# A second group of three tiles and a last unit of seven, in a chunked-attention and maxout kernel

## The chip, the cores and the metric

The kernel runs on one core of one Trainium2 chip. Its time is the device time of one execution in microseconds (us), as the median of several runs. TensorE (PE) multiplies, VectorE (DVE), ScalarE (ACT) and GpSimd (POOL) do the elementwise work, and SyncE (SP) issues every transfer between HBM and the on-chip memory. Each engine works through its own list of instructions in order and waits at an instruction until what that instruction needs is there.

## The reference

The inputs are q, k, v of shape (8, 8, 576, 64) and four weights. Attention runs inside chunks of 64 rows; its output becomes 4608 rows of 512, which go through a maximum of three products and a last product:

```python
scores = scale * np.matmul(q_c, k_c.transpose(0, 1, 2, 4, 3))   # chunks of 64
scores = scores - np.max(scores, axis=-1, keepdims=True)
attn = np.exp(scores)
attn = attn / (np.sum(attn, axis=-1, keepdims=True) + 1e-09)
x = np.matmul(attn, v_c)                        # then laid out as 4608 x 512
h = np.maximum(np.maximum(x @ w1, x @ w2), x @ w3)     # 512 -> 768
out = h @ w_out                                        # 768 -> 512
```

## The kernel before

The 4608 rows are 36 tiles of 128. The first eight tiles are two plain groups of four (`GROUPS = [4, 4]`); the other 28 are four units of 6, 8, 8 and 6 tiles (`UNITS`). Every fp32 product is made of three matmuls on a high and a low part of each operand (`three`, lines 173 to 176).

A plain group makes 18 products (six column blocks j of the 768, three weights w), each 4 x 3 matmuls of 128 x 512, and then projects each tile with 6 x 3 matmuls of 128 x 512. A unit multiplies by Winograd's form of Strassen's rule: 7 block products where the plain way has 8. Per unit there are 9 sets (three pairs of j, three w) of 7 products of 2 x 3 matmuls, and 7 x 2 x 3 x 3 matmuls of projection, 504 in all, each as wide as half a unit: 384 columns for six tiles, 512 for eight.

The units need weights that are mixed beforehand, once: for each of the 9 sets GpSimd adds the high and low parts back together (`f`, two instructions on line 370) and makes four sums and differences (`c`, four instructions on line 383); ScalarE casts `c` to its high part (`s`, line 388), VectorE makes the low part (line 391), and two transfers write `s` to HBM (line 405). The mixing runs beside the end of the first group and the whole second group. `f` and `c` have one buffer each, so a set's first `c` waits until VectorE has read the last one's.

When the second group's 18 products are done, the early pools are given up (`change`), and the memory that held weights and `s` holds the units' operands: X1 to X7 (line 503 the high part on ScalarE, line 507 the low part on VectorE, lines 498 the mixes), the sums `kept`, and the ring of weights loaded back from HBM (line 529). The first write of X1 therefore waits for the last transfer of mixed weights.

Attention is spread between the matmuls: S (scores, line 227), T (transposes, line 253) and V (values, line 265) of later tiles are inserted on TensorE; the softmax between them runs on VectorE, ScalarE and, in the last insertion of a stretch, GpSimd (line 191 divides by the sum; T waits for it).

The order is set in two ways. `FIRST` is a list written by hand for the first group (M in it starts the clock of the mixing). From there on a planner counts a nominal time `now` along TensorE's steps, and everything else is put down with a due time by `plan` and is emitted when `now` has passed it. The due times only set the order on each engine; on the chip an instruction runs when its waits are over.

Of the kernel before, what the change touches and what calls it, by code (L numbers as in the profile page):

```python
# [9 lines left out]
F32 = mybir.dt.float32  # L10
# [10 lines left out]
P = 128  # L21
# [3 lines left out]
SCALE = 1.0 / float(D) ** 0.5  # L25
GROUPS = [4, 4]
UNITS = [6, 8, 8, 6]
PAIRED = sum(GROUPS)
HALF = 512
# [6 lines left out]
OPERANDS = 0.94  # L36
MIX = 0.52

# [17 lines left out]
X51 A52 Y50p W65 K11 exp6 B60 A61 Y42 F32f h40f hh3f nrm5 h41f B63 C52 H51 V4 S7 A60 hl3f sum6 Y51 v6 W62 C60 F40f mx7  # L56
C61 X52p T5 X60 h42f H52 X61 H60 A62 xh4 h50f eps6 h51f Y60 K00 Y52p F41f A64 F42f P10 K12 hh4f H61 at5 C62 C64 K01
A63 xl4 h52f sub7 X64 B65 hl4fp K22 B62 exp7 P30 Y61 C63 V5 rec6 F50f X63p nrm6p T6 sum7 eps7 P20 K20 F51f X62p A65
rec7 C65 F52f P31 hh5f H62 xh5 v7 nrm7p Y62 at6 H63 hl5fp P21 Y63 T7 P22 P00 H64 K10 P23 P32 xl5 P01 X65 M at7 H65 P11
V6 V7 q8 q9 P12 xh6 xh7 xl6 P02 Y64 P13 xl7 Y65 P33 P34 P14 P35 P24 P03 P25 P04 K21 O2 P15 P05 K02 O0 O3 O1  # L60
"""
# [3 lines left out]
def chunk_attn_maxout_kernel(  # L65
# [48 lines left out]
    for name in FIRST.split():  # L114
        k = (3 * int(name[1]) + int(name[2])) if name[0] in "WAXY" else None
        if name[0] == "W":
            words_in[k] = free.pop(0)
# [86 lines left out]
    def plain_steps(t, x_of, col):  # L204
# [83 lines left out]

    def moe(t0, x_of, banks_in=((ps_m, "pm"),)):

# [57 lines left out]
        def hidden(j, w):  # L348
            for ct, _ in enumerate(products(j, w, 0, 512)):
                yield [] if ct < CT - 1 else [(0.3, lambda: maximum(j, w, 0, 512))] + (  # L350
                [(2.08, lambda: high(j, 0, 512)), (2.13, lambda: low(j, 0, 512))] if w == 2 else [])

# [7 lines left out]
    def store(n):  # L360
# [42 lines left out]
        def mixed():  # L403
            for k in range(2):
# [68 lines left out]
    def unit(t0, count, rooms):  # L473
# [35 lines left out]
        def operands():  # L509
            return [(0.0, high(1)), (0.39, low(1)), (2.71, mix(5, b12, b11, nc.vector)), (3.48, high(5)),  # L510
                    (3.31, mix(6, b22, source[5], nc.vector)), (8.01, mix(7, b22, b12, nc.gpsimd)), (3.37, high(6)),
                    (7.69, low(6)), (7.41, high(2)), (7.89, low(5)), (10.85, mix(4, b21, source[6], nc.gpsimd)), (7.67, low(2)),
                    (8.42, high(7)), (8.79, low(7))]

# [74 lines left out]
        def hidden(n, loads):  # L589
# [31 lines left out]
            if w == 2:  # L621
# [17 lines left out]
                def less(eng, out, x, y):  # L639
# [9 lines left out]
                             (5.31 * f, high(7)), (6.98 * f, low(7)), (6.27 * f, high(6)), (7.95 * f, low(6)),  # L649
                             (7.98 * f, high(4)), (8.86 * f, low(4))]  # L650
            for i in ORDER:
# [75 lines left out]
    idle = hpool.tile([P, 1024], mybir.dt.bfloat16, name="h", tag="h5")  # L727
    g0 = moe(0, lambda: x_tiles(0))
# [5 lines left out]
    for t in range(8):  # L734
        ops.update((f"{n}{t}", fn) for n, fn in plain_steps(t, lambda i=t // 4: x_tiles(i), t % 4 * P).items())
    for c, (lo, hi) in columns.items():
# [10 lines left out]
    mixing = [store(n) for n in range(len(sets))]  # L747
    for t in (8, 9):
        begun[t] = plain_steps(t, stage, (t - 8) * P)
        ops[f"q{t}"] = begun[t]["q"]  # L750

# [265 lines left out]
```

## Time and profile before

| | |
|---|---|
| three runs | 613.76, 614.07, 614.53 us, median 614.07 |
| profiled execution | 614.42 us, of which the span of the engines is 612.6 |
| TensorE | 605.4 us busy, 99% of the span, 5107 matmuls |
| VectorE, ScalarE, GpSimd | 432.5, 271.4, 291.1 us busy |
| granted TensorE clock | 1.0 of full speed over the span |

The profile is of one execution. Times in it count from the start of the span. TensorE's busy time is modelled at the ends of matmuls, so a step is read from the distance of two starts, not from the duration of one. The chain of waits goes back from the last instruction to whatever released each one; where it runs through other engines for a while, TensorE had no slack against them there, or nearly none.

In the profile's time the first group ends at 94.2 us, the second group's products at 154.2, its projection at 171.5, and the units fill the rest.

### The profile page before, as it was taken

What the parts mean: (1) busy time and instruction counts of PE and PEld (TensorE: products, weight loads), DVE (VectorE), ACT (ScalarE), POOL (GpSimd) and SP (SyncE); (2) the same over time, 40 slices, a digit from 0 to 9 for tenths busy, and PEclk for the clock granted to TensorE, in tenths of its full rate; (3) what the DMA queues carried; (4) which work ended last, traced back from release to release, by engine and by line L of the source; (5) the groups of instructions that cost most, each with busy time, mean ns of one, the idle gap of its engine ahead of it and who ended that gap; (6) DMA issues with size and microseconds to landing.
All of it is one profiled execution on the core that took longest, in us unless ns stands there. A gap on an engine that the chain in (4) does not pass through costs nothing.

```text
span 612.6 us, 12709 instructions
## 1 busy us (share of the span) xinstructions
PE 605.4 (99%) x5107; PEld 526.5 (86%) x5107; DVE 432.5 (71%) x678; ACT 271.4 (44%) x483; POOL 291.1 (48%) x241
## 2 busy tenths in 40 slices
PE   8999999999999999999999999999999999999997
PEld 4788888888899999998888887888888888999997
DVE  5899954687657988794595859863868387375752
ACT  5888643344444554544252535432434252242440
POOL 3553478884257775454262624532534234242430
PEclk9999999999999999999999999999999999999999
DMA  8986849687988997889585748497566657977774
GB/s 320 359 336 207 286 162 355 240 306 274 346 311 294 345 365 270 287 299 353 187 287 178 276 152 278 156 331 285 175 200 207 201 173 260 324 251 243 242 231 177
DMA packets 54219, 161.26 MB, mean 263 GB/s; under 512 B 4880, under 2 KB 16144, under 8 KB 49168
## 3 DMA queue, kind: packets, MB, share of 16 engines
q1 hardware_dynamic: 54160, 160.45, 74.6%
q8 instruction: 40, 0.66, 0.4%
q14 instruction: 19, 0.16, 0.1%
HBM read 128.97 MB, written 31.46 MB: 262 GB/s over the span
## 4 chain that ended last, share of the span: by engine, by line
PE 88%; DVE 4%; DMA 3%; ACT 2%; issue 1%; POOL 0%; SPq 0%; ACTq 0%; POOLq 0%; DVEq 0%
PE pm L586 65%; PE pm L174 5%; PE pm L175 5%; PE pm L176 5%; DMA buf<-in_qk 2%; PE s L227 2%; PE s L265 1%; PE y L265 1%; DMA w<-s 1%; PE y L227 1%; PE s L253 1%; PE tp L253 1%; PE y L253 1%; PE pm L755 1%; ACT X L503 1%
## 5 line engine op out<-in xcount | busy, mean ns | idle before, releaser
L586 PE MATMUL pm<-X,ring 128*128 128x512 f32 (+1 forms) x1512 | 310.9, 364 | 0.2 <-ACT kept L600 0.2
L586 PEld LDWEIGHTS pm<-X,ring 128*128 128x128 f32 x1512 | 271.3, 188 | 30.5 <-ACT kept L600 0.5
L600 ACT COPY kept<-pm 128x384 f32<-128x384 f32 (+1 forms) x108 | 57.1, 533 | 139.3 <-PE pm L586 101.2
L586 PE MATMUL pm<-Y,ring 128*128 128x512 f32 (+1 forms) x504 | 103.2, 363 | 0.1
L586 PEld LDWEIGHTS pm<-Y,ring 128*128 128x128 f32 x504 | 90.6, 188 | 10.4 <-DVE Y L636 0.6
L610 POOL TENSOR_TENSOR kept<-kept 128x384 f32<-128x384 f32 (+1 forms) x36 | 45.4, 1262 | 79.7 <-ACT kept L600 79.6
L597 DVE TENSOR_TENSOR most<-pm,most 128x384 f32<-128x384 f32 (+1 forms) x72 | 44.9, 623 | 51.7 <-PE pm L586 50.3
L191 POOL TENSOR_TENSOR e<-e,sm 128x512 f32<-128x512 f32 x27 | 31.8, 1177 | 62.9 <-DVE sm L188 44.2
L174 PE MATMUL pm<-xh,wl 128*128 128x512 f32 (+1 forms) x156 | 59.8, 383 | 0.0
L175 PE MATMUL pm<-xl,wh 128*128 128x512 f32 (+1 forms) x156 | 58.5, 375 | 0.3 <-DVE xl L276 0.3
L176 PE MATMUL pm<-xh,wh 128*128 128x512 f32 (+1 forms) x156 | 58.3, 373 | 0.0
L606 POOL TENSOR_TENSOR kept<-kept 128x384 f32<-128x384 f32 (+1 forms) x24 | 29.6, 1235 | 57.9 <-DVE kept L603 49.4
L636 DVE TENSOR_TENSOR Y<-most,Y 128x384 fp32r<-128x384 f32 (+1 forms) x72 | 53.7, 762 | 3.4 <-ACT Y L633 3.2
L633 ACT CAST Y<-most 128x384 fp32r<-128x384 f32 (+1 forms) x72 | 40.1, 570 | 30.3 <-DVE most L597 16.0
L241 ACT ACTIVATE e<-e 128x512 f32<-128x512 f32 x36 | 22.7, 631 | 34.4 <-DVE e L237 34.2
L603 DVE TENSOR_TENSOR kept<-pm,kept 128x384 f32<-128x384 f32 (+1 forms) x36 | 22.4, 621 | 18.3 <-PE pm L586 15.2
L603 DVE TENSOR_TENSOR pm<-pm,kept 128x384 f32<-128x384 f32 (+1 forms) x48 | 30.2, 628 | 7.1 <-PE pm L586 5.6
L175 PEld LDWEIGHTS pm<-xl,wh 128*128 128x128 f32 x156 | 29.4, 188 | 5.4 <-DVE xl L276 0.5
L176 PEld LDWEIGHTS pm<-xh,wh 128*128 128x128 f32 x156 | 29.4, 188 | 5.3
L174 PEld LDWEIGHTS pm<-xh,wl 128*128 128x128 f32 x156 | 29.4, 188 | 5.2
L182 DVE TENSOR_REDUCE sm<-e 128x8 f32<-128x512 f32 x36 | 24.5, 682 | 9.3 <-ACT e L241 8.7
L370 POOL TENSOR_TENSOR f<-wh,wl 128x512 f32<-128x512 f32 x18 | 27.3, 1539 | 2.5 <-DVE ao L163 1.8
(111 smaller groups left out, 843.7 us busy)
## 6 DMA issues: line engine op xcount, KB each, us to landing
ring<-w SPq DMA_DIRECT2D x36, 1024.0 KB, 5.5
ring<-w SPq DMA_DIRECT2D x36, 768.0 KB, 5.8
ring<-wo SPq DMA_DIRECT2D x28, 768.0 KB, 4.9
buf<-in_qk SPq DMA_DIRECT2D x36, 512.0 KB, 6.5
buf<-in_vb SPq DMA_DIRECT2D x36, 256.0 KB, 5.0
w<-s SPq DMA_DIRECT2D x18, 512.0 KB, 4.5
out_t<-ao SPq DMA_DIRECT2D x16, 256.0 KB, 3.9
stage<-in_w SPq DMA_DIRECT2D x7, 512.0 KB, 6.2
```

The costliest lines, as they stand in the source:

```text
L174: nc.tensor.matmul(out=o, lhsT=al, rhs=bh, start=first, stop=False)
L175: nc.tensor.matmul(out=o, lhsT=ah, rhs=bl, start=False, stop=False)
L176: nc.tensor.matmul(out=o, lhsT=ah, rhs=bh, start=False, stop=last)
L191: eng.tensor_tensor(out=e, in0=e, in1=sm.unsqueeze(2).broadcast_to([P, 8, 64]), op=ALU.mult)
L586: nc.tensor.matmul(out=o[i], lhsT=a, rhs=b, start=new and k == 0, stop=last and k == 2, skip_group_check=i in banks_of_product)
L597: return lambda: nc.vector.tensor_tensor(out=M(k, c), in0=of(), in1=M(k, c), op=most)
L600: return lambda: nc.scalar.copy(out=kept(k), in_=o[i])
L603: return lambda: nc.vector.tensor_tensor(out=out(), in0=o[i], in1=kept(k), op=plus)
L606: nc.gpsimd.tensor_tensor(out=kept(1) if w else M(1, 1), in0=kept(3), in1=kept(1), op=plus)
L610: (0.0, lambda: nc.gpsimd.tensor_tensor(out=kept(2), in0=kept(2), in1=kept(0), op=plus))],
L633: return lambda: nc.scalar.copy(out=y_room(i, jp)[:, 0, :half], in_=t[i]())
L636: return lambda: nc.vector.tensor_tensor(out=y_room(i, jp)[:, 1, :half], in0=t[i](), in1=y_room(i, jp)[:, 0, :half].bitcast(F32), op=minus)
```

## The change

One tile goes from the second group to the last unit: groups of 4 and 3, units of 6, 8, 8 and 7. The second group's products are then 384 columns wide and its projection has three tiles. Tile 7 keeps its attention in the first group and goes straight into the first unit's stage; the scores of tiles 8 and 9 move from the second group into the first (`S8 S9` behind `P33`), and their softmax with them.

The mixing of set 0 (`G0` to `G8`) stands in `FIRST` now, and M comes earlier. `f` and `c` have two places each, for even and odd sets. The planned distance of sets goes from 6.94 to 6.6, and within a set the high part, low part and store from 4.86, 5.79 and 8.77 to 9.0, 10.0 and 12.6. The second group has three insertions with values, of which the third lies ahead of the end of the products. The operands of the first unit have new due times, X2 early. Two loads of the projection's weights go to other buffers.

```diff
-GROUPS = [4, 4]
-UNITS = [6, 8, 8, 6]
+GROUPS = [4, 3]
+UNITS = [6, 8, 8, 7]
 # FIRST, one line of it before and after
-rec7 C65 F52f P31 hh5f H62 xh5 v7 nrm7p Y62 at6 H63 hl5fp P21 Y63 T7 P22 P00 H64 K10 P23 P32 xl5 P01 X65 M at7 H65 P11
+rec7 C65 F52f P31 hh5f H62 xh5 v7 nrm7p G2 G3 Y62 at6 H63 hl5fp G4 G5 M P21 Y63 T7 P22 P00 H64 K10 P23 P32 xl5 P01 X65 at7 H65 G6 P11
...
-            st["s"] = s = home(PAIRED)[:, :, t % 2 if t < 6 else 0]
+            st["s"] = s = (bank_of("ps_s") if t == 8 else home(PAIRED))[:, :, t % 2 if t < 6 else int(t == 8)]
...
         def hidden(j, w):
-            for ct, _ in enumerate(products(j, w, 0, 512)):
+            n = count * P
+            for ct, _ in enumerate(products(j, w, 0, n)):
...
-                    st["f"] = att.tile([P, 2, CT, P], F32, name="f", tag="qs", bufs=1)
+                    st["f"] = (att if n % 2 else xp).tile([P, 2, CT, P], F32, name="f", tag=("f", "qs")[n % 2], bufs=1)
...
-                    st["c"] = att.tile([P, 4, 256], F32, name="c", tag="rv", bufs=1)
+                    st["c"] = (att if n % 2 else xp).tile([P, 4, 256], F32, name="c", tag=("c", "rv")[n % 2], bufs=1)
...
-                (3.79, sum_of(3, a12, sums(0), minus)), (4.86, high), (5.79, low), (8.77, mixed)]
+                (3.79, sum_of(3, a12, sums(0), minus)), (9.0, high), (10.0, low), (12.6, mixed)]
...
     def stores():
-        for n in range(len(sets)):
+        for n in range(1, len(sets)):
             for at, fn in mixing[n]:
-                plan(now + MIX + 6.94 * n + at, 0.0, fn)
+                plan(now + 2.0 + 6.6 * (n - 1) + at, 0.0, fn)
...
     def first_tiles(time):
-        own, nexts = [[]] + pairs[0], pairs[0] + [pairs[1][0]]
-        lead = 8.84
-        gap = (time - lead - 0.5) / (len(own) - 1)
-        for i, (values, scores) in enumerate(zip(own, nexts)):
+        chain = [(8.84, [1, 2], [3, 4]), (24.6, [3, 4], [5]), (time - 4.9, [5], pairs[1][0])]
+        for n in (1, 2):
+            transposes(n, now + 4.0 + 0.7 * n)
+        for at, values, scores in chain:
...
-    parts += [("steps", lambda: g["project"](0, 1)), ("steps", lambda: g["project"](2)), ("steps", lambda: g["project"](3))]
+    parts += [("steps", lambda: g["project"](0, 1)), ("steps", lambda: g["project"](2))]
```

GpSimd at the end of the first group, before: the last low part of a group's `h`, then the first two sets.

```order
L325 TENSOR_TENSOR h<-m,h 128x512
L163 TENSOR_TENSOR ao<-ao,stage 128x512
L191 TENSOR_TENSOR e<-e,sm 128x512
L163 TENSOR_TENSOR ao<-ao,stage 128x512
L191 TENSOR_TENSOR e<-e,sm 128x512
L325 TENSOR_TENSOR h<-m,h 128x512
L370 TENSOR_TENSOR f<-wh_114,wl_120 128x512
L370 TENSOR_TENSOR f<-wh_115,wl_121 128x512
L383 TENSOR_TENSOR c<-f 128x256
```

The same place in the changed kernel:

```order
L372 TENSOR_TENSOR f<-wh_114,wl_120 128x512
L372 TENSOR_TENSOR f<-wh_115,wl_121 128x512
L326 TENSOR_TENSOR h<-m,h 128x512
L164 TENSOR_TENSOR ao<-ao,stage 128x512
L192 TENSOR_TENSOR e<-e,sm 128x512
L164 TENSOR_TENSOR ao<-ao,stage 128x512
L192 TENSOR_TENSOR e<-e,sm 128x512
L385 TENSOR_TENSOR c<-f 128x256
L385 TENSOR_TENSOR c<-c,f 128x256
L326 TENSOR_TENSOR h<-m,h 128x512
L385 TENSOR_TENSOR c<-f 128x256
L385 TENSOR_TENSOR c<-f,c 128x256
```

Set 0's `f` stands ahead of the first `h` and its four `c` around the last one, so set 1 begins behind them instead of set 0.

ScalarE where the second group's products end, before: the last set's high part (`s`), then the last copies, X1 and the last `h`.

```order
L388 CAST s<-c 128x4x256
L314 COPY m<-pm 128x512
L258 COPY xs<-y 128x512
L258 COPY xs<-s 128x512
L279 COPY stage<-y 128x2x4x64
L279 COPY stage<-s 128x2x4x64
L241 ACTIVATE e<-e 128x512
L503 CAST X_2055<-stage 128x2x384
L322 CAST h<-m 128x512
L241 ACTIVATE e<-e 128x512
```

And in the changed kernel:

```order
L390 CAST s<-c 128x4x256
L315 COPY m<-pm 128x384
L242 ACTIVATE e<-e 128x512 x2
L505 CAST X_2010<-stage 128x2x384
L505 CAST X_2013<-stage 128x2x384
L323 CAST h<-m 128x384
L505 CAST X_2045<-most 128x2x384
```

Two X casts (X1 and X2) now stand ahead of the last `h` of the second group.

VectorE behind that place in the changed kernel; tile 14's sum, guard and reciprocal (`sm`) are the rows between.

```order
L509 TENSOR_TENSOR X_2010<-stage,X_2010 128x2x384
L183 TENSOR_REDUCE sm<-e 128x8
L186 TENSOR_SCALAR sm<-sm 128x8
L326 TENSOR_TENSOR h<-m,h 128x384
L500 TENSOR_TENSOR most<-stage 128x2x384
L189 RECIPROCAL sm<-sm 128x8
```

Before, the reciprocal of the last tile of this stretch stood farther behind X1's low part, and its T lay 54 matmuls into a projection of 72; in the changed kernel T13 and T14 lie 21 and 36 matmuls into a projection of 54.

## Rows read from the trace of the kernel before

**Rows 1.** The page: busy time of the engines (share of span, count).

```profile
PE 605.4 (99%) x5107; PEld 526.5 (86%) x5107; DVE 432.5 (71%) x678; ACT 271.4 (44%) x483; POOL 291.1 (48%) x241
```

**Rows 2.** What TensorE waited for: us in total, times, longest.

```profile
PE pm L586 <- ACT kept L600: 0.2, 1, 0.2
```

**Rows 3.** Timeline of TensorE, 33 to 45 us: start, us, instruction.

```profile
33.34 0.39 PE L175 MATMUL pm<-xl,wh 128*128 128x512 f32 x1
...
44.22 0.39 PE L175 MATMUL pm<-xl,wh 128*128 128x512 f32 x1
```

**Rows 4.** The chain that ended last, pieces on TensorE: start, us, what.

```profile
103.22 0.62 PE y L227 x32
103.84 0.47 PE s L227 x32
...
114.06 0.44 PE y L253 x4
...
188.36 5.21 PE pm L586 x30
...
415.89 22.50 PE pm L586 x99
```

**Rows 5.** Timeline of TensorE where the second group's parts begin and end.

```profile
94.21 0.39 PE L174 MATMUL pm<-xh,wl 128*128 128x512 f32 x1
...
154.17 0.39 PE L174 MATMUL pm<-woh,h 128*128 128x512 f32 x1
```

**Rows 6.** Timeline of GpSimd, 77 to 147 us, idle time before in brackets.

```profile
77.99 1.75 POOL L325 TENSOR_TENSOR h<-m,h 128x512 fp32r<-128x512 f32 x1
81.57 2.54 POOL L370 TENSOR_TENSOR f<-wh,wl 128x512 f32<-128x512 f32 x2 [1.83 <-DVE ao L163]
...
87.32 3.33 POOL L370 TENSOR_TENSOR f<-wh,wl 128x512 f32<-128x512 f32 x2
91.87 0.74 POOL L383 TENSOR_TENSOR c<-f 128x256 f32<-128x256 f32 x1 [1.22 <-DVE s L391]
...
118.80 2.27 POOL L370 TENSOR_TENSOR f<-wh,wl 128x512 f32<-128x512 f32 x1
...
146.04 0.74 POOL L383 TENSOR_TENSOR c<-f 128x256 f32<-128x256 f32 x1
```

**Rows 7.** Timeline of VectorE, two of the low parts of mixed weights.

```profile
89.41 2.31 DVE L391 TENSOR_TENSOR s<-c,s 128x1024 fp32r<-128x1024 f32 x1
...
118.59 1.34 DVE L391 TENSOR_TENSOR s<-c,s 128x1024 fp32r<-128x1024 f32 x1 [2.41 <-ACT s L388]
```

**Rows 8.** Groups on GpSimd, 81.5 to 147 us: busy, mean ns, idle before.

```profile
L383 POOL TENSOR_TENSOR c<-f 128x256 f32<-128x256 f32 x18 | 14.5, 803 | 7.1 <-DVE s L391 4.3 <-DVE sm L188 1.3 <-DVE sm L185 1.2
```

**Rows 9.** The chain that ended last, 148 to 158 us.

```profile
148.49 1.06 ACT s L388
...
149.57 1.24 DVE s L391
...
151.19 5.79 DMA w<-s
...
157.08 0.84 ACT X L503
...
157.94 0.96 DVE X L507
```

**Rows 10.** Transfers issued from 91 to 93 us: count, size, median us to landing.

```profile
w<-s SPq DMA_DIRECT2D x2, 512.0 KB, 3.1
```

**Rows 11.** Timeline of VectorE and GpSimd behind X1, 159 to 166 us.

```profile
159.49 0.68 DVE L325 TENSOR_TENSOR h<-m,h 128x512 fp32r<-128x512 f32 x1
...
163.23 0.68 DVE L182 TENSOR_REDUCE sm<-e 128x8 f32<-128x512 f32 x1
...
164.15 0.20 DVE L188 RECIPROCAL sm<-sm 128x8 f32<-128x8 f32 x1
...
164.52 1.04 POOL L191 TENSOR_TENSOR e<-e,sm 128x512 f32<-128x512 f32 x1 [3.02 <-DVE sm L188]
```

More of the change, by code (lines that the diff above doesn't have):

```diff
@@ L25 @@
 SCALE = 1.0 / float(D) ** 0.5
-GROUPS = [4, 4]
-UNITS = [6, 8, 8, 6]
-PAIRED = sum(GROUPS)
+GROUPS = [4, 3]
+UNITS = [6, 8, 8, 7]
+PAIRED = 8
 HALF = 512
@@ L36 @@
 OPERANDS = 0.94
-MIX = 0.52
 FIRST = """
@@ L56 @@
 X51 A52 Y50p W65 K11 exp6 B60 A61 Y42 F32f h40f hh3f nrm5 h41f B63 C52 H51 V4 S7 A60 hl3f sum6 Y51 v6 W62 C60 F40f mx7
[L57 removed]
+C61 X52p T5 X60 h42f H52 X61 H60 A62 xh4 h50f eps6 h51f Y60 K00 Y52p G0 G1 F41f A64 F42f P10 K12 hh4f H61 at5 C62 C64 K01
 A63 xl4 h52f sub7 X64 B65 hl4fp K22 B62 exp7 P30 Y61 C63 V5 rec6 F50f X63p nrm6p T6 sum7 eps7 P20 K20 F51f X62p A65
[L59 to L60 removed]
+rec7 C65 F52f P31 hh5f H62 xh5 v7 nrm7p G2 G3 Y62 at6 H63 hl5fp G4 G5 M P21 Y63 T7 P22 P00 H64 K10 P23 P32 xl5 P01 X65 at7 H65 G6 P11
+V6 V7 q8 q9 G7 P12 K02 xh6 x7 xl6 P02 Y64 P13 v8 v9 P33 S8 S9 mx8 Y65 sub8
+P34 exp8 G8 P14 mx9 q10 sum8 sub9 P35 exp9 q11 P24 eps8 rec8 nrm8 P03 sum9 P25 P04 eps9 O2 rec9 nrm9 P15 P05 K21 O0 O3 O1
 """
@@ L116, in chunk_attn_maxout_kernel @@
         if name[0] == "W":
-            words_in[k] = free.pop(0)
+            at = next((i for i, n in enumerate(free) if 3 < n < 7), 0) if name in ("W62", "W65") else 0
+            words_in[k] = free.pop(at)
         elif name[0] == "A":
@@ L287, in chunk_attn_maxout_kernel, with moe @@
     outputs = []
-    def moe(t0, x_of, banks_in=((ps_m, "pm"),)):
+    def moe(t0, x_of, count, banks_in=((ps_m, "pm"),)):
         hh, hl = [None] * JT, [None] * JT
@@ L348, in hidden @@
         def hidden(j, w):
-            for ct, _ in enumerate(products(j, w, 0, 512)):
-                yield [] if ct < CT - 1 else [(0.3, lambda: maximum(j, w, 0, 512))] + (
-                [(2.08, lambda: high(j, 0, 512)), (2.13, lambda: low(j, 0, 512))] if w == 2 else [])
+            n = count * P
+            for ct, _ in enumerate(products(j, w, 0, n)):
+                yield STEP_H[2 * count], [] if ct < CT - 1 else [(0.3, lambda: maximum(j, w, 0, n))] + (
+                    [(2.08, lambda: high(j, 0, n)), (2.13, lambda: low(j, 0, n))] if w == 2 else [])
         return dict(products=products, maximum=maximum, high=high, low=low, hidden=hidden, project=project, places=places,
@@ L509, in operands @@
         def operands():
[L510 to L513, printed above, removed]
+            return [(0.0, high(1)), (0.35, low(1)), (0.4, high(2)), (1.2, mix(5, b12, b11, nc.vector)),
+                    (2.0, mix(6, b22, source[5], nc.vector)), (2.15, high(5)), (2.2, mix(7, b22, b12, nc.gpsimd)), (2.9, low(2)),
+                    (3.0, high(6)), (3.9, low(5)), (4.9, low(6)), (5.0, high(7)), (5.0, mix(4, b21, source[6], nc.gpsimd)),
+                    (6.0, low(7)), (6.5, high(3)), (7.0, low(3)), (7.6, high(4)), (8.2, low(4))]
         def operands_behind():
@@ L649, in hidden @@
                              (5.31 * f, high(7)), (6.98 * f, low(7)), (6.27 * f, high(6)), (7.95 * f, low(6)),
-                             (7.98 * f, high(4)), (8.86 * f, low(4))]
+                             (7.98 * f, high(4)), (8.5 * f, low(4))]
             for i in ORDER:
@@ L727, in chunk_attn_maxout_kernel @@
     idle = hpool.tile([P, 1024], mybir.dt.bfloat16, name="h", tag="h5")
-    g0 = moe(0, lambda: x_tiles(0))
+    g0 = moe(0, lambda: x_tiles(0), GROUPS[0])
     total = (3 * JT * CT + 4 * JT) * STEP + 4 * TILE
@@ L733, in chunk_attn_maxout_kernel @@
         ops.update((f"{n}{j}{w}", fn) for n, fn in piece(j, w).items())
-    for t in range(8):
-        ops.update((f"{n}{t}", fn) for n, fn in plain_steps(t, lambda i=t // 4: x_tiles(i), t % 4 * P).items())
+    for t in range(PAIRED + 4):
+        steps_ = plain_steps(t, lambda i=t // 4: x_tiles(i), t % 4 * P)
+        if t >= sum(GROUPS):
+            steps_ = begun[t] = plain_steps(t, stage, (t - sum(GROUPS)) * P)
+        ops.update((f"{n}{t}", fn) for n, fn in steps_.items())
     for c, (lo, hi) in columns.items():
@@ L747, in chunk_attn_maxout_kernel @@
     mixing = [store(n) for n in range(len(sets))]
-    for t in (8, 9):
-        begun[t] = plain_steps(t, stage, (t - 8) * P)
-        ops[f"q{t}"] = begun[t]["q"]
+    ops.update((f"G{k}", fn) for k, (_, fn) in enumerate(mixing[0]))
     def idle_products(n):
@@ L809, in chunk_attn_maxout_kernel @@
     groups, parts = [g0], []
-    g = moe(starts[1], lambda: x_tiles(1))
+    g = moe(starts[1], lambda: x_tiles(1), GROUPS[1])
     groups.append(g)
@@ L854, in insertion @@
         for k, n in enumerate(values):
-            plan(at - loads + 0.38 * k, 0.0, lambda n=n: steps(n)["v"]())
+            if sum(GROUPS) + n not in (8, 9):
+                plan(at - loads + 0.38 * k, 0.0, lambda n=n: steps(n)["v"]())
             plan(at + 1.41 + 0.58 * k, 0.0, lambda n=n: steps(n)["x"]())
@@ L861, in first_tiles @@
     def first_tiles(time):
-        own, nexts = [[]] + pairs[0], pairs[0] + [pairs[1][0]]
-        lead = 8.84
-        gap = (time - lead - 0.5) / (len(own) - 1)
-        for i, (values, scores) in enumerate(zip(own, nexts)):
-            last = i == len(own) - 1
-            insertion(values, scores, now + lead + gap * i, 11.6, nc.gpsimd if last else nc.vector,
-                      (0.7, 4.6) if last else (0.2, 3.02), (10.9, 10.9) if last else (10.1, 9.4))
+        chain = [(8.84, [1, 2], [3, 4]), (24.6, [3, 4], [5]), (time - 4.9, [5], pairs[1][0])]
+        for n in (1, 2):
+            transposes(n, now + 4.0 + 0.7 * n)
+        for at, values, scores in chain:
+            last = values == [5]
+            insertion(values, scores, now + at, 11.6, nc.gpsimd if last else nc.vector,
+                      (0.7, 4.6) if last else (0.2, 3.02), (10.9, 10.9) if last else (8.9,) if scores == [5] else (10.8, 9.6))
     def tiles(u, time):
@@ L876, in tiles @@
         nexts = own[1:] + (pairs[u + 1][:1] if u + 1 < len(pairs) else [[]])
-        lead = 20.93 if u == 1 else 19.96
+        lead = 16.84 if u == 1 else 19.96
         gap = (time - 10.53 - lead) / (len(own) - 1)
@@ L929, in stores_out @@
             for at, fn in store_out(jp):
-                plan(now + 22.0 + 17.12 * jp + at, 0.0, fn)
-    inner = 3 * JT * CT * STEP + UNITS[0] * TILE
+                plan(now + 17.9 + 17.12 * jp + at, 0.0, fn)
+    inner = 3 * JT * CT * STEP_H[2 * GROUPS[1]] + 5 * TILE
+    outer = GROUPS[1] * JT * STEP
     def span(u):
@@ L940, in chunk_attn_maxout_kernel @@
     parts += [("steps", lambda j=j, w=w: g["hidden"](j, w)) for j in range(JT) for w in range(3)]
-    parts += [("do", change), ("do", lambda: operands(0, OPERANDS)), ("do", lambda: last_operands(0, 4 * JT * STEP + 0.0)),
+    parts += [("do", change), ("do", lambda: operands(0, OPERANDS)),
               ("do", stores_out),
-              ("do", lambda: tiles(1, 4 * JT * STEP + span(0))), ("do", lambda: load(0, 0, 1.72, 1.35)), ("do", lambda: load(0, 1, 2.31, 5.13))]
-    parts += [("steps", lambda: g["project"](0, 1)), ("steps", lambda: g["project"](2)), ("steps", lambda: g["project"](3))]
+              ("do", lambda: tiles(1, outer + span(0))), ("do", lambda: load(0, 0, 1.72, 1.35)), ("do", lambda: load(0, 1, 2.31, 5.13))]
+    parts += [("steps", lambda: g["project"](0, 1)), ("steps", lambda: g["project"](2))]
     parts.append(("do", lambda: places.__setitem__(slice(None), g["places"])))
```

## The prediction

> **What bounds the kernel now.** I read the page first: TensorE is busy for 605.4 of 612.6 us [rows 1], so a time is won by fewer or narrower matmuls, and lost by any wait that the change puts in front of them. The waits of TensorE come second: after the first 26 us there is one, 0.2 us for ScalarE where unit 0 begins [rows 2]. The chain of waits comes third, and it is the warning: between 148 and 158 us it isn't on TensorE but runs through the mixing of the last set, ScalarE's high part, VectorE's low part, the store, and X1 behind its landing [rows 9]. So the mixing of weights ends just in time before unit 0. The reader is to see that the second group is the time in which this mixing is hidden, and that the change makes this cover shorter.
>
> **What TensorE gains.** A 512-column matmul of the plain group takes (44.22 - 33.34) / 48 = 0.2267 us [rows 3]; one of 384 columns takes 5.21 / 30 = 0.1737 and one of 512 in a unit 22.50 / 99 = 0.2273 [rows 4]. Half way between the last two, 448 columns cost 0.2005, an estimate.
> - Products of the second group: 18 x 12 = 216 matmuls, each 0.0530 less: -11.4 us.
> - Its projection: 18 matmuls less at 0.2267: -4.1.
> - The last unit: 504 matmuls, each 0.0268 more: +13.5.
> - Attention is the same 36 tiles. A group of inserted pieces costs a little beside them: the second group spans 59.96 us [rows 5], of which 216 x 0.2267 = 48.97 are matmuls and 9.8 are pieces (S8 and S9, three fours of V and S at 0.62 + 3 x 0.47, six T at 0.44 [rows 4]), so 1.2 us over ten changes. There is one more such group: +0.2, between 0.1 and 0.4.
> - The wait of 0.2 us [rows 2] belongs to the old place: -0.2.
>
> The sum is -2.0 us where nothing new waits. The clock was full throughout, and I leave it so.
>
> **When the products need the mixed weights.** In the changed order S8 and S9 (1.1 us) go into the first group, so the second group begins at 94.2 + 1.2 = 95.4 us. Its 216 matmuls take 37.5 us, the pieces in it (T8 to T12 at 0.44, a four at 2.03 and two threes at 1.56) 7.3, seven changes 0.8: the projection begins at 141.1 us instead of 154.2, 13 us sooner. T14 stands 36 matmuls into it: 141.1 + 8.2 + 0.6 = 149.9 us.
>
> **When they are ready.** Here the cover is spent. GpSimd needs six instructions a set. From set 1's first at 87.32 to the last of set 8 at 146.78 it took 59.5 us for eight sets [rows 6]. Of this, 7.1 us were waits of the first `c`, 6.8 of them for VectorE [rows 8]; two buffers take those away. But what VectorE did in them was mostly the low part of the set before (five of the eight times), and where this ran beside GpSimd's `f`, GpSimd paid as much: the `f` at 118.80 lasted 2.27 us beside the low part at 118.59, where a pair undisturbed lasts 2.54 [rows 6, 7]. That is 1.0 us lost. With two buffers GpSimd never rests, so every low part meets one of its instructions. I take five more collisions of 1.0 us: 59.5 - 6.8 + 5.0, less 0.5 because the low parts of `h` are a quarter narrower, is 57.2 us for sets 1 to 8. The bounds are 52.7 (no collision costs anything more) and 59.5 (nothing is won).
>
> The Trainium skill has a rule for it: SBUF — State Buffer, Who interferes with whom, says that a VectorE instruction with two inputs in SBUF and a GpSimd instruction that reads SBUF exclude each other for a whole instruction, and that whichever issues first blocks the other. By it all eight low parts cost GpSimd their run, the 57.2; without it the sum for the sets would be 52.7. The rows at 118 us agree with it.
>
> Set 0's `f` moves into idle time of GpSimd before 70 us and costs nothing there. Its four `c` go ahead of set 1: from the end of the division before `h` (78.0, the start of the row at 77.99) four `c` of 0.8, the `h` of 1.75 and about 1.0 of collisions bring set 1 to 84.0 us, 3.3 sooner than 87.32 [rows 6, 8]; 82.9 without collisions, 84.5 with one more. So the last `c` of set 8 ends at 84.0 + 57.2 = 141.2 us, 5.6 sooner than 146.78, where TensorE arrives 13 us sooner. The high part 1.06 and the low part 1.24 follow, then the issue of two transfers (0.4, the gap between the low part's end and 151.19) [rows 9]. The landing took 5.8 us beside other stores [rows 9] and 3.1 where the queue was empty [rows 10]; the stores of the projection's weights are issued sooner now, so I take 4.0. With 0.1 for hand-overs X1 can be written at 141.2 + 6.8 = 148.0 us.
>
> **What waits for that.** X1's high part (0.84) and low part (0.96) [rows 9], the sum of tile 14 (0.7), its guard (0.2), the low part of the last `h` (0.6 net), a mix of X's size (0.9), the reciprocal and the hand-over (0.4, from 164.15 to 164.52) and GpSimd's division (1.04) [rows 11] stand one behind the other in front of T14. With 0.1 for hand-overs that is 5.7 us: 153.7 against 149.9, so TensorE stands 3.8 us. The last products onto the projection need the low `h` at about 148.0 + 3.4 = 151.4 and are met at 148.5, which is 2.9 of the same 3.8 and not added to them. Tile 9's transposed copy on ScalarE is queued behind the high part of set 3 in the same way; set 3 ends at 84.0 + 3 x 7.15 = 105.5, the high part and the copy (0.6) at 107.1, V9 is met at 105.5. These 1.6 us are an instalment of the same sum, as GpSimd's end doesn't move with TensorE. A stop and start costs another 0.2. Behind T14 the other needs (X2 on the bank of X1, the ring) are late by less.
>
> The sum: -2.0 + 3.8 + 0.2 = +2.0 us on the profiled execution's 614.42, 616.4. That execution lies 0.35 above the median of 614.07, so I predict 616.1.
>
> Other edits at no cost: the new operand order of X2 to X7 lies in the 10 us between X1 (148.0) and the later begin of unit 0 (154.4 + 4.0), where before it had 14.4 (157.08 to 171.5); the new buffers for two weight loads are free in the first group; the softmax of tiles 8 and 9 begins behind S9 at 89.1 us and has some 8 us of VectorE with two low parts of weights (an estimate from the durations in rows 9 and 11), T8 comes at 100.6. If one of these covers is gone, it costs 0.5 to 1.5 us, within the range.
>
> **The rivals.**
> - *The sets do close up* to 52.7 us, 6.6 each. For it: the 6.8 us of waits are real, and some low parts beside GpSimd cost VectorE instead, as at 89.41, 2.31 us long [rows 7]. Then set 8 ends at 84.0 + 52.7 = 136.7, X1 can start at 143.5, and T14 is met at 149.2, before its 149.9. Nothing waits: 614.07 - 2.0 = 612.1. This is the other side. Against it: VectorE's long one at 89.41 only waited for the end of an `f`, and then ran while GpSimd was stopped by its own wait.
> - *Half of it*: collisions cost GpSimd 0.5 on average, set 8 ends at 138.7, T14 is late by 1.3: 614.07 - 2.0 + 1.3 + 0.2 = 613.6, no change that can be told.
> - *The full delay*: set 1 starts at 84.5, eight sets take 59.0, the landing 5.8. X1 at 152.1, T14 late by 7.9: 620.2.
>
> **How the numbers follow.** A change of 0.2% (1.2 us) is about what a measurement of this kernel can tell. The forecast, set 8 late by lock-step with VectorE, has 0.50 and its own range is 614.6 to 618.6; a tenth of it lies within 0.2%. The closed-up sets have 0.22, the half 0.18, the full delay 0.10. So faster 0.22; same 0.18 + 0.05 = 0.23; slower 0.45 + 0.10 = 0.55. The range goes from 611.8, which takes in the closed-up case, to 619.0, where about a tenth is left above.
>
> **What would show it.** In the profile after: matmuls of 384 columns at 0.174 in the second group and of 448 at 0.200 in the last unit (if not, the gain is wrong). GpSimd's rows of `f` and `c` without waits, but with `f` of 2.2 us beside low parts; the last `c` of set 8 near 141 (at 137 the rival is right). TensorE waiting for T's input, the last `h` or tile 9's values between 104 and 155, some 4 us together, and nothing of size in the units. I am wrong in kind if TensorE has no wait there, or if the time is lost in the first group or in the last unit.

## The result, and the profile after

The changed kernel takes 619.26 us (median of 4 runs, 619.14 to 619.5), the kernel before 613.91 in the same comparison: a ratio of 1.0086, 95% interval 1.0068 to 1.0103. It is slower by 5.35 us, where I forecast 616.1 (slower by 2.0) with a range up to 619.0.

The page of the changed kernel: busy time, share of the span and count, and the shares of the chain that ended last. The span is 617.5 us (execution 619.29).

```profile
PE 606.5 (98%) x5087; PEld 527.5 (85%) x5089; DVE 444.8 (72%) x676; ACT 273.5 (44%) x482; POOL 305.2 (49%) x242
...
PE 77%; DVE 10%; POOL 5%; ACT 3%; issue 3%; DMA 1%; SPq 0%; POOLq 0%; ACTq 0%; DVEq 0%
```

Against [rows 1], TensorE is busy for 1.1 us more in a span that is 4.9 longer: 3.8 us more are idle. What TensorE waited for most behind the first 26 us (us in total, times, longest), where [rows 2] had one wait of 0.2:

```profile
PE y L254 <- POOL e L192: 1.1, 1, 1.1
PE pm L175 <- ACT ao L338: 1.0, 1, 1.0
...
PE y L254 <- DVE e L192: 0.8, 1, 0.8
PE pm L175 <- DVE h L326: 0.3, 1, 0.3
```

These are, in this order, T14, the second group's first product, T12, and the last products onto the projection. Lines are shifted by one or two against the kernel before. TensorE's timeline (start, us, instruction, in brackets the idle time before):

```profile
97.03 0.44 PE L175 MATMUL pm<-xh,wl 128*128 128x384 f32 x1 [1.01 <-ACT ao L338]
...
144.57 0.39 PE L175 MATMUL pm<-woh,h 128*128 128x512 f32 x1
...
155.18 0.66 PE L254 MATMUL y<-ident,e 128*128 128x128 f32 x4 [1.11 <-POOL e L192]
...
511.78 8.47 PE L588 MATMUL pm<-X,ring 128*128 128x448 f32 x41
...
599.74 14.35 PE L588 MATMUL pm<-Y,ring 128*128 128x448 f32 x70
```

The projection begins at 144.57 where I had 141.1, and T14 comes at 155.18 against a place of 149.9. The last unit runs from 511.78 to 614.09, 102.3 us for 504 matmuls. The same unit before:

```profile
521.68 18.61 PE L586 MATMUL pm<-X,ring 128*128 128x384 f32 x106
...
599.76 9.52 PE L586 MATMUL pm<-Y,ring 128*128 128x384 f32 x54
```

That is 521.68 to 609.28, 87.6 us: 14.7 us more for the seventh tile, 0.2030 us a matmul of 448 columns. GpSimd in the changed kernel, beside [rows 6]:

```profile
84.26 3.53 POOL L372 TENSOR_TENSOR f<-wh,wl 128x512 f32<-128x512 f32 x2
...
101.67 1.59 POOL L385 TENSOR_TENSOR c<-f 128x256 f32<-128x256 f32 x1
...
139.99 0.74 POOL L385 TENSOR_TENSOR c<-f 128x256 f32<-128x256 f32 x1
...
153.51 1.61 POOL L192 TENSOR_TENSOR e<-e,sm 128x512 f32<-128x512 f32 x1 [6.72 <-PE pm L177]
```

Set 1 starts at 84.26 and the last `c` of set 8 ends at 140.73: 56.5 us, no wait in between, but `f` pairs of up to 3.53 (2.54 undisturbed) and `c` of up to 1.60 (0.74). What follows, from the chain that ended last (start, us, what), beside [rows 9]:

```profile
141.15 0.61 DVE mx L233
...
142.40 1.23 DVE s L393
...
143.64 0.32 SPq L407
...
145.30 3.89 DMA buf<-in_vb
...
149.27 0.84 ACT X L505
...
150.14 0.96 DVE X L509
```

The low part stands behind tile 13's maximum and subtraction, and X1 comes 5.65 us after the low part's end. The releaser named is a tile load that was issued just behind the two stores.

GpSimd isn't what every high part of a set waits for. Set 5's last `c` ended at 119.38 and set 7's at 133.92, but their high parts on ScalarE began 2.6 and 2.1 us later, behind a copy that waited for VectorE's low part of `h`. ScalarE's timeline at set 5:

```profile
121.57 0.48 ACT L315 COPY m<-pm 128x384 f32<-128x384 f32 x1 [3.28 <-DVE h L326]
121.94 1.06 ACT L390 CAST s<-c 128x1024 fp32r<-128x1024 f32 x1
```

### The profile page after: what moved, and what is told of

Read it like the earlier page. It is cut to its first block, busy times and chain, and to the rows that moved or that the text cites. A ratio compares the mean times of both kernels' runs of the same rounds, so it can differ in the third digit from the quotient of the medians.

```text
span 617.5 us, 12662 instructions
## 1 busy us (share of the span) xinstructions
PE 606.5 (98%) x5087; PEld 527.5 (85%) x5089; DVE 444.8 (72%) x676; ACT 273.5 (44%) x482; POOL 305.2 (49%) x242
## 4 chain that ended last, share of the span: by engine, by line
PE 77%; DVE 10%; POOL 5%; ACT 3%; issue 3%; DMA 1%; SPq 0%; POOLq 0%; ACTq 0%; DVEq 0%
PE pm L588 67%; POOL c L385 2%; POOL f L372 2%; PE s L228 1%; DVE h L326 1%; PE s L266 1%; PE pm L176 1%; PE pm L175 1%; PE pm L177 1%; DVE s L393 1%; DVE m L317 1%; DVE ao L164 1%; PE y L266 1%; DVE sm L183 1%; PE y L228 1%
## 5 line engine op out<-in xcount | busy, mean ns | idle before, releaser
L588 PE MATMUL pm<-X,ring 128*128 128x512 f32 (+2 forms) x1512 | 322.6, 372 | 0.2 <-ACT kept L602 0.2
L602 ACT COPY kept<-pm 128x512 f32<-128x512 f32 (+2 forms) x108 | 58.6, 548 | 126.2 <-PE pm L588 72.3
L588 PE MATMUL pm<-Y,ring 128*128 128x512 f32 (+2 forms) x504 | 106.9, 371 | 0.1
L612 POOL TENSOR_TENSOR kept<-kept 128x512 f32<-128x512 f32 (+2 forms) x36 | 47.4, 1316 | 90.3 <-ACT kept L602 90.2
L599 DVE TENSOR_TENSOR most<-pm,most 128x512 f32<-128x512 f32 (+2 forms) x72 | 46.0, 640 | 50.5 <-PE pm L588 49.0
L608 POOL TENSOR_TENSOR kept<-kept 128x512 f32<-128x512 f32 (+2 forms) x24 | 30.7, 1279 | 56.8 <-DVE kept L605 48.2
L638 DVE TENSOR_TENSOR Y<-most,Y 128x512 fp32r<-128x512 f32 (+2 forms) x72 | 54.4, 770 | 5.7 <-ACT Y L635 5.4
L175 PE MATMUL pm<-xh,wl 128*128 128x384 f32 (+2 forms) x156 | 55.6, 356 | 1.0 <-ACT ao L338 1.0
L635 ACT CAST Y<-most 128x512 fp32r<-128x512 f32 (+2 forms) x72 | 41.0, 583 | 33.1 <-DVE most L599 16.5
L176 PE MATMUL pm<-xl,wh 128*128 128x384 f32 (+2 forms) x156 | 54.4, 349 | 0.3 <-DVE xl L277 0.3
L177 PE MATMUL pm<-xh,wh 128*128 128x384 f32 (+2 forms) x156 | 54.3, 348 | 0.0
```

The source lines that it names most:

```text
L175: nc.tensor.matmul(out=o, lhsT=al, rhs=bh, start=first, stop=False)
L176: nc.tensor.matmul(out=o, lhsT=ah, rhs=bl, start=False, stop=False)
L177: nc.tensor.matmul(out=o, lhsT=ah, rhs=bh, start=False, stop=last)
L588: nc.tensor.matmul(out=o[i], lhsT=a, rhs=b, start=new and k == 0, stop=last and k == 2, skip_group_check=i in banks_of_product)
L599: return lambda: nc.vector.tensor_tensor(out=M(k, c), in0=of(), in1=M(k, c), op=most)
L602: return lambda: nc.scalar.copy(out=kept(k), in_=o[i])
```

## The experiments

Where nothing else is said, the edit is made to the changed kernel. Each ratio (with its 95% interval) is against the kernel before, run beside it. Places in two traces compare to about half a us: set 0's `f` starts between 63.96 and 64.89 in the traces of the changed kernel and its variants.

**e1_land.** Is X1 held by the landing of the last set's store? The late rooms, X1 among them, lie on the memory that the weights and `s` give back, so the first write waits for all its readers. Set 8 alone gets other rooms:

```diff
+            if n == len(sets) - 1:
+                st["s"] = [att.tile([P, 4, 256], F32R, name="s", tag=tag, bufs=1) for tag in ("qs", "rv")]
...
```

> Based on the changed kernel (619.3 us). The mixed parts of the last set only go into two 4 KB rooms of the memory that stays (those of f and c, free by then), so that X1 no longer waits for the landing of that set's store. Theory A (the chain behind GpSimd's last c, with its landing of 5 us, is what the projection's part of the second group waits for; the earlier waits of TensorE are instalments of the same delay): X1 at about 143.8 instead of 149.27, T14's input ready at about 150, so the waits of 0.35 before P and 1.11 before T14 go and nothing else does: 617.8, between 617.3 and 618.3. Rival B (X1 is held by something else that comes at the same time: the tile loads or TensorE's last reading): X1 stays at 149, time 619.3. Rival C (TensorE's whole lateness hangs on this chain, so that the early waits go as well): 615.5.

Measured 616.97 (1.0042, 1.003 to 1.0054), 2.3 us less, a little more than the 1.0 to 2.0 that theory A gave. ScalarE's timeline, and TensorE's:

```profile
146.51 0.63 ACT L242 ACTIVATE e<-e 128x512 f32<-128x512 f32 x1 [3.08 <-DVE e L238]
147.05 1.55 ACT L513 CAST X<-stage 128x768 fp32r<-128x768 f32 x2
...
144.83 0.39 PE L175 MATMUL pm<-woh,h 128*128 128x512 f32 x1
...
153.53 0.60 PE L254 MATMUL y<-ident,e 128*128 128x128 f32 x4
```

X1 waits for no landing any more, and the waits before the last `h` (0.35) and T14 (1.11) are gone, and one of 0.2 where unit 0 begins; rival B falls. It comes at 147.05 and not at 143.8, because tile 14's exponential stands ahead of it. The projection still begins at 144.83, so rival C falls too: the landing explains what is lost behind the projection's start, not what is lost ahead of it.

**e2_early and e3_both.** Are the early waits losses of their own?

```diff
-P34 exp8 G8 P14 mx9 q10 sum8 sub9 P35 exp9 q11 P24 eps8 rec8 nrm8 P03 sum9 P25 P04 eps9 O2 rec9 nrm9 P15 P05 K21 O0 O3 O1
+P34 exp8 G8 P14 mx9 q10 sum8 sub9 P35 q11 P24 eps8 rec8 nrm8 P03 P25 O2 exp9 sum9 P04 eps9 rec9 nrm9 P15 P05 K21 O0 O3 O1
...
-                      (0.7, 4.6) if last else (0.2, 3.02), (10.9, 10.9) if last else (8.9,) if scores == [5] else (10.8, 9.6))
+                      (0.7, 4.6) if last else (0.2, 3.02), (10.9, 10.9) if last else (9.9,) if scores == [5] else (10.8, 9.6))
```

> Based on the changed kernel (619.3 us). Order only: the first output copy of the first group stands ahead of tile 9's exponential on ScalarE, and tile 12's transposes stand 1 us later in the second group, so that the two largest early waits of TensorE (1.0 at 97.0, 0.8 at 133.5) go. Theory A (instalments: GpSimd's chain and not TensorE's place fixes T14 at 155.2): TensorE arrives at the projection 1.8 us sooner and waits as much more before the last h and T14: 619.3, between 619.0 and 619.6. Rival D (these waits are losses of their own, of ScalarE's and VectorE's order): 617.5.

> Based on the changed kernel (619.3 us). Both edits: the last set's parts outside the memory that X1 needs, and the two early waits taken away by order. Theory A: each takes away what the other can't, the waits of 1.0, 0.8, 0.35 and 1.11 all go: 616.0, between 615.5 and 616.8. If the early waits were instalments of something behind T14 as well (X2 to X7 on ScalarE and VectorE), time stays at 617.5. Rival D: as e1_land less 1.8.

e2: 619.28 (1.0083, 1.0069 to 1.0097), no change; rival D falls. Its waits of TensorE:

```profile
PE s L266 <- ACT xs L259: 1.4, 1, 1.4
PE y L254 <- POOL e L192: 1.1, 1, 1.1
PE y L266 <- ACT xs L259: 1.0, 2, 0.8
```

The waits didn't go to T14, as I had expected, but to V9 and V12. e3 took 616.74 (1.0039, 1.0027 to 1.0051): inside the expected numbers, but for another reason: the early waits moved to V9 and V12 there too, the projection begins at 144.81 as before, and only T14's wait is gone.

**e4_one_input and e5_scalar_low.** Is it the meetings with VectorE's low part?

```diff
-            nc.vector.tensor_tensor(out=st["s"][:, :, 1], in0=st["c"], in1=st["s"][:, :, 0].bitcast(F32), op=minus)
 # e4
+            nc.vector.tensor_copy(out=st["s"][:, :, 1], in_=st["c"])
 # e5
+            nc.scalar.copy(out=st["s"][:, :, 1], in_=st["c"])
```

Both leave out the subtraction of the high part.

> Based on the changed kernel (619.3 us). VectorE's low part of the mixed weights is made by a copy of c instead of the subtraction of the high part (the subtraction is left out for these parts): same engine, same place in its queue, same size, but one input from SBUF instead of two. Theory L (the lock: an instruction of VectorE with two SBUF inputs and one of GpSimd keep each other out): GpSimd's f pairs of 3.5 beside low parts fall to 2.54 and its c of 1.6 to 0.74, the last c of set 8 ends at 133 to 136 instead of 140.7, and T14's wait goes: 616.5 to 618. Rival M (VectorE and GpSimd merely share bandwidth, or GpSimd's own speed sets it): f and c beside the copies stay as long, last c at 140 or later, 619.3.

> Based on the changed kernel (619.3 us). The low part of the mixed weights is made by a copy of c on ScalarE, in VectorE's stead (the subtraction of the high part is left out for these parts); VectorE has no instruction on c any more. In the run with a one-input copy on VectorE GpSimd still paid about 0.4 us a meeting (c of 1.06 instead of 0.74, f pairs of 2.97), the last c of set 8 ended at 136.7 and the time was 614.0. Theory L (any VectorE instruction that runs beside holds GpSimd up, ScalarE's don't): c(8) ends at 132 to 135, the f and c that are still long are those beside the low parts of h, the divisions and the subtractions of the softmax; time 614.0, since nothing was waited for any more. Rival M (traffic of any engine on the same memory): as long as with the copy, c(8) at 136.7 or later.

e4: 614.01 (0.9996, 0.9987 to 1.0005), below the 616.5 to 618 that I expected, since all the waits of TensorE went and not T14's alone; e5: 613.56 (0.9992, 0.9983 to 1.0001), about the 614.0 expected. The last `c` of set 8 in e4, and GpSimd in e5:

```profile
135.66 1.04 POOL L385 TENSOR_TENSOR c<-f 128x256 f32<-128x256 f32 x1
...
84.34 2.53 POOL L372 TENSOR_TENSOR f<-wh,wl 128x512 f32<-128x512 f32 x2
...
132.51 0.75 POOL L385 TENSOR_TENSOR c<-f 128x256 f32<-128x256 f32 x1
```

Sets 1 to 8 take 48.9 us with the low parts on ScalarE, 52.4 (84.31 to 136.70) with a one-input copy on VectorE, 56.5 with the subtraction. So a low part costs GpSimd 7.6 / 8 = 0.95 us, and a copy still costs 3.5 / 8 = 0.44: rival M falls, and so does the clean form of L in which one input is free. TensorE in e5:

```profile
95.63 0.33 PE L175 MATMUL pm<-xh,wl 128*128 128x384 f32 x1
...
141.09 0.39 PE L175 MATMUL pm<-woh,h 128*128 128x512 f32 x1
...
149.78 0.60 PE L254 MATMUL y<-ident,e 128*128 128x128 f32 x4
...
154.36 4.35 PE L588 MATMUL pm<-X,ring 128*128 128x384 f32 x24
```

These are the places that I had worked out for TensorE without waits (95.4, 141.1, 149.9, 154.4). All of the changed kernel's new waits have gone, the early ones too. e5 takes work from VectorE as well as meetings from GpSimd; e11 below tells the two apart.

**e6_one_buffer, e7_set0_sooner, e8_three.** What do the second buffers bring, and does an earlier start help?

```diff
 # e6, and c likewise
-                    st["f"] = (att if n % 2 else xp).tile([P, 2, CT, P], F32, name="f", tag=("f", "qs")[n % 2], bufs=1)
+                    st["f"] = xp.tile([P, 2, CT, P], F32, name="f", tag="f", bufs=1)
...
 # e7
-C61 X52p T5 X60 h42f H52 X61 H60 A62 xh4 h50f eps6 h51f Y60 K00 Y52p G0 G1 F41f A64 F42f P10 K12 hh4f H61 at5 C62 C64 K01
+C61 X52p T5 X60 h42f H52 X61 H60 A62 xh4 h50f eps6 h51f Y60 K00 Y52p G0 G1 F41f A64 F42f P10 K12 G2 G3 G4 G5 hh4f H61 at5 C62 C64 K01
...
-rec7 C65 F52f P31 hh5f H62 xh5 v7 nrm7p G2 G3 Y62 at6 H63 hl5fp G4 G5 M P21 Y63 T7 P22 P00 H64 K10 P23 P32 xl5 P01 X65 at7 H65 G6 P11
+rec7 C65 F52f P31 hh5f H62 xh5 v7 nrm7p Y62 at6 H63 hl5fp M P21 Y63 T7 P22 P00 H64 K10 P23 P32 xl5 P01 X65 at7 H65 G6 P11
```

e8 is e1, e2 and e7 together.

> Based on the changed kernel (619.3 us). Only the two buffers for f and c are undone: one room for each, so GpSimd waits again for VectorE's low part before the first c of the next set. Theory L (what GpSimd saved in waits it pays in meetings with low parts, so the buffers bring 1 to 2.5 us over eight sets): c(8) ends at 142 to 143.2 instead of 140.7, the time is 620.3 to 621.8. Rival (the buffers bring the whole 6.8 us of waits that the trace of the kernel before showed): c(8) at 147.5, time 626.

> Based on the changed kernel (619.3 us). Order on GpSimd only: the four c of set 0 stand right behind its f, at 67.7 us, where GpSimd is idle for 3.4 us, instead of among the divisions and the low h from 78.7 on; set 1 then starts at about 81 instead of 84.3. Theory A (the second group of TensorE goes in step with GpSimd's sets): every set ends 3 us sooner, c(8) at 137.5, and TensorE's waits of 1.0, 0.8, 0.35 and 1.1 shrink by about 3 us in all: 616.4, between 615.8 and 617.2. Rival (the sets are held by what VectorE and ScalarE give, not by GpSimd's start): c(8) at 140, time 619.

> Based on the changed kernel (619.3 us). The three order and room edits together: last set's parts outside the memory of X1, the first output copy ahead of tile 9's exponential and T12 1 us later, set 0's four c sooner. Theory A: what is left of TensorE's waits after the last of these goes, unit 0 begins at about 155 as with the one-input copy: 614.3, between 613.8 and 615.2, which is the kernel before within 0.2%; it can't go below that, since TensorE's own work only shrank by 0.8 (the 448-column matmul took 0.2030, not 0.2005). Rival: the low parts meet GpSimd as before and the waits move to another place: 616.

e6: 620.6 (1.0106, 1.0092 to 1.0119). GpSimd in e6, the first `f` of set 1, the longest wait and the last `c`:

```profile
83.80 3.52 POOL L372 TENSOR_TENSOR f<-wh,wl 128x512 f32<-128x512 f32 x2
...
117.12 0.74 POOL L385 TENSOR_TENSOR c<-f 128x256 f32<-128x256 f32 x1 [1.95 <-DVE s L393]
...
142.61 0.73 POOL L385 TENSOR_TENSOR c<-f 128x256 f32<-128x256 f32 x1
```

Its sets 1 to 8 take 59.5 us with 7.4 us of waits for VectorE in five places. With two buffers these waits are gone, but the sets take 56.5: 3.1 us shorter, and the rest is paid in meetings. The time is 1.3 us shorter.

e7: 619.37 (1.0085, 1.007 to 1.0099), a miss for theory A, and the time that the rival gave. Set 1 started only 2.3 us sooner (81.94), and TensorE paid for it. VectorE's timeline in e7, two shifts of weights beside the moved `c`:

```profile
70.34 2.41 DVE L160 TENSOR_SCALAR ao<-ao 128x512 uint32<-128x512 uint32 x2
```

and in the changed kernel, where GpSimd was idle:

```profile
70.24 0.75 DVE L160 TENSOR_SCALAR ao<-ao 128x512 uint32<-128x512 uint32 x2
```

The 1.66 us are handed on to tile 6's division, and TensorE waits for it in the first group:

```profile
77.90 0.65 PE L254 MATMUL tp<-ident,e 128*128 128x128 f32 x4 [1.58 <-POOL e L192]
```

At the other end, the last `c` of set 8, its low part and X1 in e7:

```profile
137.39 1.72 POOL L385 TENSOR_TENSOR c<-f 128x256 f32<-128x256 f32 x1
...
142.03 1.22 DVE L393 TENSOR_TENSOR s<-c,s 128x1024 fp32r<-128x1024 f32 x1
...
149.28 1.58 ACT L505 CAST X<-stage 128x768 fp32r<-128x768 f32 x2 [2.79 <-DMA buf<-in_vb]
```

The last `c` ends at 139.11, 1.6 us sooner than in the changed kernel, but the low part ends only 0.4 sooner and X1 begins at the same 149.28: the high part and the low part stand behind other work of ScalarE and VectorE. So in e7 GpSimd's end isn't what X1 waits for.

e8: 616.56 (1.0041, 1.0028 to 1.0053), a miss against 614.3 and no better than e1.

**e9_copies_first and e10_x1_first.** Does each place of ScalarE's queue hold TensorE alone? In e3, two copies of transposed weights stood behind high parts of sets.

```diff
 # e9, on e3
-            plan(at + 2.27, 0.0, lambda: steps(n)["at"]())
+            plan(at + {2: 1.0, 5: 0.2}.get(n, 2.27), 0.0, lambda: steps(n)["at"]())
...
 # e10, on e9
-OPERANDS = 0.94
+OPERANDS = 0.6
```

> Based on the kernel with both edits (last set's parts outside the memory of X1; first output copy ahead of tile 9's exponential and T12 later; 616.7 us). There the early waits of TensorE had not gone but moved: 1.4 us before V9 and 0.8 before V12, each for a copy of transposed weights on ScalarE that is queued behind the high part of a set, which waits for GpSimd's last c. Here these two copies stand ahead of the high parts of sets 3 and 7, order only. Theory A2 (TensorE is tied to GpSimd's sets by the places of ScalarE's queue where a high part stands ahead of something TensorE needs; T14 is the last such place): V9 and V12 don't wait, the second group ends 2.2 us sooner, and T14, whose input is ready at 152.9 as before, is waited for by 1.4 to 1.6 us: 616.0, between 615.6 and 616.5. Rival E (the chain before T14 moves with TensorE, since tile 14's scores come from it): nothing waits at T14 and the time is 614.5.

> Based on the kernel with the copies first. X1's high part stands ahead of tile 14's exponential on ScalarE, 0.34 us earlier in the plan, order only; the exponential waits for VectorE's subtraction until about 146, X1 only for TensorE's last reading of the weights and the end of set 7's store. Theory A2: X1 at about 145 instead of 146.6, T14's input about 1 us sooner, at 151.9; time 0.7 to 1.2 below the kernel with the copies first: 615.1. Rival: the exponential comes 0.8 later and tile 14's softmax with it, no gain: 616.0. By either it stays above the kernel before.

e9: 616.68 (1.0045, 1.0031 to 1.0059); e10: 616.99 (1.0047, 1.0035 to 1.006). Neither helps, and both lie above what I expected (615.6 to 616.5, and 615.1). TensorE in e9:

```profile
120.17 0.63 PE L254 MATMUL s<-ident,e 128*128 128x128 f32 x4 [1.76 <-DVE e L192]
...
137.73 0.69 PE L266 MATMUL y<-xs,buf 64*64 64x64 f32 x32 [0.85 <-ACT xs L259]
```

V9's wait has gone and T11's has come, for a division on VectorE that stands behind a set's low part (115.63, 1.77 us). The edit didn't do what it was for at V12: that copy (137.09) still stood behind set 7's high part (136.14). The projection begins at 144.60. In e10 X1 came at 144.92, as expected, but T14 had not been waited for in e9, so nothing was won.

**e11_more_pool.** GpSimd's pace, or VectorE's? On e5, GpSimd alone gets more to do:

```diff
-                (3.79, sum_of(3, a12, sums(0), minus)), (9.0, high), (10.0, low), (12.6, mixed)]
+                (3.79, sum_of(3, a12, sums(0), minus)),
+                *[(4.08, sum_of(2, a11, a21, minus))] * ((n > 0) + (n in (3, 6))), (9.0, high), (10.0, low), (12.6, mixed)]
```

> Based on the kernel whose low parts are ScalarE copies (the subtraction of the high part is left out there; 613.6 us, sets 1 to 8 in 48.9 us, projection from 141.1, no wait of TensorE). GpSimd repeats one c of each of sets 1 to 8 once and of two sets twice (ten instructions of 0.74, nothing else changed), so that its last c ends at about 140.6, as in the changed kernel, while VectorE has no two-input instruction on c. Theory G (TensorE's second group goes at the pace of GpSimd's sets, through the high parts in ScalarE's queue): the early waits come back, the projection starts at 143 to 144.6, T14 is waited for, and the time is 617 to 619. Rival V (it goes at the pace of VectorE, whose softmax the meetings make longer; GpSimd's own end matters only for X1): the projection starts at 141.1 to 141.8, only the waits before the last h and T14 come back, larger (T14's input at about 154 against a place of 150): 617 to 618 too, but with all of its wait behind the projection's start. The place of the wait tells them apart, not the time.

618.21 (1.0068, 1.0055 to 1.008). The last `c` of set 8, and TensorE:

```profile
139.51 1.55 POOL L385 TENSOR_TENSOR c<-f 128x256 f32<-128x256 f32 x2
...
107.32 0.69 PE L266 MATMUL s<-xs,buf 64*64 64x64 f32 x32 [1.88 <-ACT xs L259]
...
137.01 0.69 PE L266 MATMUL y<-xs,buf 64*64 64x64 f32 x32 [0.81 <-ACT xs L259]
...
143.88 0.39 PE L175 MATMUL pm<-woh,h 128*128 128x512 f32 x1
...
153.87 0.66 PE L254 MATMUL y<-ident,e 128*128 128x128 f32 x4 [1.12 <-POOL e L192]
```

The last `c` ends at 141.06, 0.3 us later than in the changed kernel. With no low part on VectorE at all, a slower GpSimd alone brings back 4.65 of the 5.7 us between e5 and the changed kernel, most of it ahead of the projection (2.8 of 4.1 us at T14), and VectorE is no busier for it: 31.3 us between 84 and 141 us, 32.8 in e5, 43.4 in the changed kernel. So GpSimd's pace is enough to make the early waits, and rival V falls as it was put. That it makes all of them in the changed kernel isn't shown: there VectorE's low parts stand in the same path, as set 5 and e7 show.

## Why the prediction was wrong by 3.2 us, step by step

- **The kind was right.** TensorE's own work shrinks a little, GpSimd's mixing can't follow a shorter second group, the meetings with VectorE's low parts keep the sets from closing up, and the time grows. The closed-up and half-way rivals didn't come about.
- **TensorE without waits.** Right to 0.3 us up to unit 0, as e5 shows. Unit 0 begins 17.1 us sooner there, as worked out.
- **448 columns, mis-sized.** I took half the way between two measured widths, 0.2005 us; it measured 0.2030. 504 x 0.0025 = 1.3 us. So the sum without new waits is not -2.0 but about -0.7, and e5 bears it out: -0.5.
- **GpSimd's sets.** Set 1 at 84.26 (forecast 84.0), eight sets in 56.5 (57.2), the last `c` at 140.73 (141.2). A low part cost 0.95 (a collision was put at 1.0). The Trainium skill (SBUF — State Buffer, Who interferes with whom) also counts copies and tensor_scalar among the instructions that can take the ports VectorE shares with GpSimd. The traces agree: e4's copies cost 0.44 each, and e7's shifts took 2.41 us in place of 0.75.
- **From the last `c` to X1, the step that failed.** I summed 6.8 us; it took 8.54 (140.73 to 149.27). The low part ended 2.89 us after the `c` instead of 2.3, as VectorE had tile 13's softmax in front of it, a wait that the sum put at nothing (in e7 it ended 4.1 us after the `c`), and X1 came 5.65 behind that, where I had 0.4 for the issue, 4.0 for the landing and 0.1. With the upper bound of the landing, 5.8 [rows 9], the 5.65 would have been 6.3: nearer than my 4.5, which leaned on the empty queue's 3.1 [rows 10].
- **From X1 to T14.** 5.91 against 5.7: the division ran beside VectorE and took 1.61, not 1.04. With the two, T14 is 5.3 us late instead of 3.8, and unit 0 begins at 159.78 instead of 158.4.
- **Where the wait shows.** I named one early instalment, 1.6 at V9, and the rest in front of T14. In fact 3.5 us are lost ahead of the projection and 1.9 behind it. TensorE is tied to the sets in more than one place: by ScalarE's high part, which at sets 1 to 4 waits for the last `c`, and by VectorE's low part. Taking one early place away (e2, e9) moved the wait to another; shorter sets (e4, e5) took all of them away, and longer ones (e11) brought most of the time back. For the sum the place matters little, since T14 is late by X1's chain wherever the early waits lie (155.18 in the changed kernel and in e2).
- **What is left.** 1.3 + 1.4 is 2.7 of the 3.2 us. Of the rest, 0.2 is left to the units by difference, and 0.3 are the 0.35 that I took off because the profiled execution of before lay above its median: that of the changed kernel lies only 0.03 above its own.

What stays open is a version that beats the kernel before: the best, without VectorE's low parts (e5), is 0.5 us below it, within what can be told, and it leaves work out. Why T12's and T11's places trade the same 1 to 2 us under every order was shown in its effect, not followed to the last instruction. How the changed kernel's waits divide between GpSimd's pace and VectorE's longer list is open too.

## What to carry to other kernels

Where a stage is shortened that hides another engine's work, ask for the pace of that work at every step that shares an in-order queue with the stage, and not for its end alone. Here removing early waits by order bought nothing (e2, e9), freeing the last one bought 2.3 us (e1), and only less work in the sets took all of them away (e4, e5). A second buffer between VectorE and GpSimd turns waits into meetings when both read SBUF: here 7.4 us of waits went, the sets became 3.1 us shorter and the kernel 1.3. Where two terms of a sum are taken between rows that lie apart, as the width of 448 and the landing were, both can miss the same way: here by 1.3 us and 1.2 (5.65 against 4.5), and the range, which ended 2.9 us above the forecast, was just too short.

## What the runs showed of the hardware

A matmul of 448 columns took 0.2030 us, 2.5 ns more than half way between 384 (0.1738) and 512 (0.2273 [rows 4]). The meetings go both ways and don't need two inputs. VectorE's copies of 128x1024 in e4, the first beside an `f` of GpSimd, the last with GpSimd at rest:

```profile
84.39 1.76 DVE L393 CAST s<-c 128x1024 fp32r<-128x1024 f32 x1 [2.57 <-POOL c L385]
...
137.36 0.68 DVE L393 CAST s<-c 128x1024 fp32r<-128x1024 f32 x1
```

The same copy on ScalarE (85.36, 1.05 us) left the `f` pair beside it at 2.53 (e5).
